# The order of the attention's steps taken from a stored list instead of a planner's rules with shifts

## The chip, the core and the metric

The kernel runs on one core of a Trainium2 chip. The time is the device time of one execution in microseconds (us), the median of three runs. The engines are TensorE (PE, matrix products; its weight loads are shown as PEld), VectorE (DVE), ScalarE (ACT), GpSimd (POOL) and SyncE (SP, which here only issues transfers). TensorE's clock has two levels, 1.2 and 2.4 GHz; the profile gives the granted clock as a share of the upper one.

## What is computed

Attention with mixed heads, and then a feed-forward layer with a softmax gate (SoLU) and a layer norm, over 4 batches, 12 heads, 448 positions, head size 64; the second part has 1792 tokens, 768 to 1024 to 768 channels.

```python
scores = scale * np.matmul(q, k.transpose(0, 1, 3, 2))
scores = np.einsum('bhij,hg->bgij', scores, w_pre)
attn = softmax(scores)                      # maximum, exp, sum + 1e-9, division
attn = np.einsum('bhij,hg->bgij', attn, w_post)
x = np.matmul(attn, v)                      # to (1792, 768)
h = x @ w_in
solu = h * softmax(h)
ln = (solu - mean) / sqrt(var + 1e-6) * g_ln
out = ln @ w_out
```

## The kernel before

Products that need more than fp16 are made of two fp16 halves, `hi` and `lo`. The attention is cut into about 2600 small steps ("tasks"), each with a key. For a batch `b`:

- `ld` loads q, k and v (`raw_q`, `raw_k`, `raw_v`). `am` takes maxima of pieces, `sc` turns them into a power-of-two scale; one step of `sc` is a pair of matmuls, `spread_q` or `spread_k`, that hands a maximum to all partitions. For batch 0 PE transposes (`tp`, line 591, tiles `pt_q`, `pt_k`) and ACT and DVE split (`th`, `tl`); for later batches `hi` (POOL) and `lo` (DVE in two instructions, line 365, or POOL in four, lines 558 and 559) split, and `t` transposes by a transfer (line 571).
- `qk` makes the scores of two heads for a block of 90 or 120 rows (line 644, tile `ps`); `sh` (ACT, line 656) and `sl` (DVE, line 661) copy them to SBUF as halves. Two banks of PSUM hold scores.
- A unit is ten rows of all twelve heads, 45 units a batch. `f` (SP, line 692) fetches a unit into `sr`, with room for four pairs of units. `m`, the premix (line 711, tile `pm`), mixes the heads of a pair of units; `mx` (DVE, line 721) takes the maximum, `ex` (ACT, line 737) the exponential, `gd` and `iv` (DVE) the reciprocal of the sum, `w` (POOL, line 758) the weights `wr`; `o`, the postmix (line 766, tile `po`), mixes again; `po` (ACT, line 369) copies it out.
- `av` (line 815, tile `px`) multiplies by v for two heads; `xh` and `xl` split the result.
- In the last batch `fw` (line 883, tile `cv_wi`) fetches w_in in pieces, `wi`, `wm`, `wh` and `wl` convert it, and `h0` starts the second part.
- 50 `warm` steps of two matmuls each (line 624) compute nothing that is used.

Each task names the engines that can take it, what it needs, and which buffers it takes and frees. `Plan.order()` simulates the engines with fixed costs and due times and gives one list of all tasks; `Plan.shifted()` then moves single tasks in it by the numbers of `SHIFT`. The tasks are written into the program in the order of that list, so each engine gets its own in that order and works through them strictly one after the other; a task that waits holds all that stand behind it on its engine. The second part has a plan of its own, `moe.order()`.

Of the kernel before, what the change touches and what calls it, by code (L numbers as in the profile page):

```python
# [18 lines left out]
class Plan:  # L19
# [34 lines left out]
    4 10 4 -3 1 12 13 1 2 3 -3 3 8 14 2 6 7 1 16 5 24 4 0 3 -11 4 7 9 14 8 9 7 -4 8 16 -5 15 -5 8 9 5 8
    16 -8 -4 15 10 14 15 4 15 1 3 13 22 14 11 14 14 0 8 21 12 20 25 13 11 12 18 4 10 13 16 24 21 0 14 10
    -35 -32 -26 -17 -94 -90 -75 -107 -71 -30 -57 -27 1 -6 0x2 4 -1 5 -1 9 5 -1 4 14 8 17 1 -4 3 4 -9 4
    -8 -3 5 -6 4 -1 7 2 8 5 5 8 5 7 7 -4 7 11 7 -1 12 5 12 13 3 5 14 17 3 4 -71 6 6 -63 -32 -23 -30 -15
    -14 -10 2 -6 1 6 -5 -4 10 11 0 -2 9 2 2 8 8 -4 -4 10 12 1 4 -15 3 -13 -7 -20 0 1 -5 3 -1 2 5 10 -3
    0x2 -3 0 3 8 8 3 -3 -5 2 -2 -1 -7 1 1 1 1 2 0 1 3 0 2 -1 2 2 4 4 0x2 2 -6 3 0 3 -1 2 -1 1 -60 1 1 3
    3 -4 5 5 7 0 3 -3 4 6 0 -5 4 1 -1 -14 1 3 0 3 -1 0 2 2 2 5 9 4 5 -6 -3 -3 2 6 -5 -3 1 1 9 1 1 7 1 1  # L60
    2 5 -4 4 8 -4 3 3 -3 8 9 0 4 0 4 -23 -2 -61 -3 -11 5 0x2 4 -4 4 -2 7 4 7 -4 8 5 -3 -3 -2 4 -9 6 2 6
    -18 1 -8 1 2 2 2 3 -11 0 2 2 2 6 9 -4 -1 -16 2 2 2 5 -6 -6 1 2 -8 -3 1 7 0 2 -4 2 8 -4 -4 -3 -1 1 5
    7 -3 3 3 4 8 -4 -10 -8 3 -1 -8 -2 -2 0x3 2 2 8 1 5 9 10 4 -2 9 -10 -10 20 2 3 4 6 7 -11 1 -8 -13 -17
# [1739 lines left out]
```

## Time and profile before

| | us |
|---|---|
| median of three runs | 652.92 |
| lowest, highest | 652.15, 654.51 |
| span of the profiled execution | 657.9 |

The page gives the profiled execution by its span, from its first to its last instruction; what lies around the span is not listed for it. Its span is 0.8% longer than the median of the timed runs. In the profile "busy" of PE includes matmuls that are under way while they wait for the ones ahead, so a stretch that is 97% busy can still hold time to be had.

### The profile page before, as it was taken

Reading aid. Unit: us, or ns where it says so; the run is one execution under the profiler, and the core shown is the slowest. Engines: PE = TensorE matmul, PEld = TensorE weight load, DVE = VectorE, ACT = ScalarE, POOL = GpSimd, SP = SyncE. Lnnn points to the kernel's source line nnn. Section 1 sums busy time; section 2 is a strip of 40 time slices with the busy share of each in tenths; the row PEclk is TensorE's granted clock in tenths of the full one; section 3 lists DMA queues with packets and bytes.
Section 4 is the critical chain, followed back from the end, with each engine's and each line's share of the span. In section 5 each row is a group of like instructions: output and inputs, shape, how many; then the busy total and the mean of one; then the engine's idle time right before and its main releaser. Section 6 shows DMA issues by size and latency. Waiting matters only on the chain.

```text
span 657.9 us, 17741 instructions
## 1 busy us (share of the span) xinstructions
PE 632.8 (96%) x6660; PEld 433.7 (66%) x6660; DVE 475.1 (72%) x1314; ACT 451.0 (69%) x981; POOL 280.1 (43%) x427
## 2 busy tenths in 40 slices
PE   6889999999999999999899999999999999999997
PEld 6647767777767778778677777774444455666664
DVE  5769998879997689997699999849889896100000
ACT  4679888989888898988799997725455576311111
POOL 2025683235844254593254246404666846300000
PEclk9779999999999999999899999999999999999999
DMA  9037578467677448788746763019964422541211
GB/s 242 12 133 229 178 152 178 156 196 221 204 185 169 150 140 236 234 175 206 219 154 221 214 224 119 3 41 295 186 160 112 97 48 57 113 113 51 64 55 48
DMA packets 114029, 98.53 MB, mean 150 GB/s; under 512 B 69604, under 2 KB 104600, under 8 KB 113944
## 3 DMA queue, kind: packets, MB, share of 16 engines
q1 hardware_dynamic: 108120, 83.62, 45.8%
q0 software_dynamic: 4416, 12.40, 6.9%
q10 hardware_dynamic: 1408, 1.38, 0.8%
q8 instruction: 52, 0.85, 0.5%
q14 instruction: 33, 0.27, 0.1%
HBM read 33.24 MB, written 9.63 MB: 65 GB/s over the span
## 4 chain that ended last, share of the span: by engine, by line
PE 64%; DVE 17%; ACT 7%; DMA 4%; issue 3%; POOL 2%; SPq 1%; ACTq 0%; DVEq 0%; POOLq 0%
PE y L1609 17%; PE po L766 15%; PE ps_h L984 12%; PE px L815 7%; PE ps L644 6%; PE pm L711 6%; DVE dead L721 4%; DVE s L661 3%; ACT e L737 3%; ACT s L656 2%; DMA raw_q<-in_q_dram 2%; DVE hl_k L365 1%; ACT p_t L369 1%; DMA sr<-s 1%; DMA cv_wi<-in_moe_w_in_dram 1%
## 5 line engine op out<-in xcount | busy, mean ns | idle before, releaser
L766 PE MATMUL po<-wr,e 128*112 128x120 f32 x1440 | 176.0, 273 | 6.4 <-POOL wr L758 4.9
L766 PEld LDWEIGHTS po<-wr,e 128*112 128x112 f32 x1440 | 156.8, 178 | 36.8 <-POOL wr L758 15.9
L758 POOL TENSOR_SCALAR wr<-wq,sm 128x120 f32<-128x120 f32 x180 | 77.1, 436 | 186.1 <-DVE sm L752 90.6
L737 ACT ACTIVATE e<-pm,nb,c_exp 128x448 f32<-128x448 f32 x180 | 131.4, 734 | 19.6 <-DVE dead L721 10.2
L721 DVE TENSOR_SCALAR_CACHE_REDUCE dead<-pm,c_nexp 128x448 f16<-128x448 f32 x180 | 121.7, 676 | 14.1 <-PE pm L711 10.1
L661 DVE SCALAR_TENSOR_TENSOR s<-ps,s 120x448 f16<-120x448 f32 (+1 forms) x192 | 112.2, 615 | 16.1 <-ACT s L656 13.8
L369 ACT COPY p_t<-po 112x480 f32<-112x480 f32 x180 | 108.2, 625 | 13.7 <-PE po L766 12.3
L656 ACT ACTIVATE s<-ps 120x448 f16<-120x448 f32 (+1 forms) x192 | 97.3, 552 | 18.1 <-PE ps L644 17.5
L815 PE MATMUL px<-p_t,raw_v 112*64 112x120 f32 (+3 forms) x1632 | 86.8, 259 | 0.8 <-ACT e L737 0.7
L815 PEld LDWEIGHTS px<-p_t,raw_v 112*64 112x64 f32 x1632 | 76.1, 137 | 16.0 <-issue 11.4
L984 PE MATMUL ps_h<-wi,xf 128*128 128x512 f16 x396 | 86.0, 379 | 0.2 <-DVE u L1536 0.2
L644 PE MATMUL ps<-k,q 64*64 64x448 f16 (+2 forms) x1008 | 79.7, 359 | 2.2 <-DVE s L661 1.5
L1609 PE MATMUL y<-wo_h,lth 128*128 128x384 f16 (+2 forms) x224 | 73.0, 326 | 0.0
L1609 PE MATMUL y<-wo_l,lth 128*128 128x384 f16 (+2 forms) x224 | 73.0, 326 | 0.0
L1609 PE MATMUL y<-wo_h,ltl 128*128 128x384 f16 (+2 forms) x224 | 73.0, 326 | 0.0
L984 PEld LDWEIGHTS <-xf 128*128 128x128 f16 x396 | 38.8, 98 | 46.8 <-issue 0.4
L1621 ACT ACTIVATE o<-y,c_out 128x384 f32<-128x384 f32 (+2 forms) x28 | 16.2, 579 | 72.7 <-PE y L1609 72.7
L1609 PEld LDWEIGHTS <-lth 128*128 128x128 f16 x448 | 43.8, 98 | 29.3
L711 PE MATMUL pm<-sr,wp_hi 64*64 64x448 f16 x720 | 57.1, 363 | 4.4 <-DMA sr<-s 2.4
L644 PEld LDWEIGHTS <-q 64*64 64x64 f16 (+2 forms) x1008 | 34.7, 107 | 24.4 <-issue 8.0
L1594 POOL TENSOR_TENSOR ll<-u,lh 128x1024 f16<-128x1024 f32 x14 | 31.4, 2245 | 15.1 <-ACT lh L1590 9.0
L737 ACT ACTIVATION_READ_ACCUMULATOR e<-pm,nb,c_exp 128x1 f32 x180 | 37.6, 209 | 0.0
(182 smaller groups left out, 800.1 us busy)
## 6 DMA issues: line engine op xcount, KB each, us to landing
sr<-s SPq DMA_DIRECT2D x176, 210.0 KB
cv_wi<-in_moe_w_in_dram SPq DMA_DIRECT2D x24, 256.0 KB
cv_wo<-in_moe_w_out_dram SPq DMA_DIRECT2D x8, 768.0 KB
raw_k<-in_k_dram POOLq DMA_DIRECT2D x18, 224.0 KB, 3.7
raw_q<-in_q_dram POOLq DMA_DIRECT2D x18, 224.0 KB, 5.4
raw_v<-in_v_dram POOLq DMA_DIRECT2D x18, 224.0 KB, 3.8
xh<-xsh SPq DMA_DIRECT2D x9, 224.0 KB
xl<-xsl SPq DMA_DIRECT2D x9, 224.0 KB
```

The costliest lines, as they stand in the source:

```text
L369: nc.scalar.copy(out=out, in_=in_)
L644: nc.tensor.matmul(sps[b, c, h + e][lo:hi], q2[b, g][rows, 2 * j + x, i0 + lo : i0 + hi], k1[b, g][rows, 2 * j + y], start=(a == 0), stop= ...
L656: nc.scalar.activation(out=s_t[b, c][0 : y.shape[0], h, 0], in_=y, func=AF.Copy, scale=2.0**-E_S)
L661: nc.vector.scalar_tensor_tensor(out=t[:, h, 1], in0=y, scalar=2.0**-E_S, in1=t[:, h, 0], op0=ALU.mult, op1=ALU.subtract)
L711: nc.tensor.matmul(pmx[b, u + i][64 * e : 64 * e + 64, 0:S], w[rows], sr[b, u][rows, e, z], start=(a == 0), stop=(a == 2),)
L721: nc.vector.tensor_scalar(out=dead, in0=pmx[b, u][:, 0:S], scalar1=c_nexp[0:UK, b : b + 1], scalar2=None, op0=ALU.mult, op1=ALU.min, accum ...
L737: nc.scalar.activation(out=ee[b, u], in_=pmx.pop((b, u))[:, 0:S], func=AF.Exp, bias=nbs.pop((b, u)), scale=c_exp[0:UK, b : b + 1], accum_o ...
L758: ENG[eng].tensor_scalar(out=w, in0=wq[0:UK, 0 : H * UN], scalar1=sm, scalar2=1.0, op0=ALU.mult, op1=ALU.mult)
L766: nc.tensor.matmul(ps[:, c * 120 : (c + 1) * 120], e[:, c * CP : (c + 1) * CP], w, start=True, stop=True)
L815: nc.tensor.matmul(xps[b, blk, g][e * 64 : e * 64 + 64, i, cut], raws["v", b, p][:, e, c * D : (c + 1) * D], next(x for y, x in block_view ...
L984: nc.tensor.matmul(ps[:, n], xx[:, kc, o : o + 128], ww[:, kc, n * 512 : (n + 1) * 512], start=(kc == 0 and a == 0), stop=(kc == KDM - 1 a ...
L1609: nc.tensor.matmul(ys[t, n], lts[t, x][:, kc], w[:, kc, c0:c1], start=(kc == 0 and a == 0), stop=(kc == KFF - 1 and a == 2),)
```

## The change

`SHIFT` is replaced by `ORDER`, a list of 2629 numbers, and `shifted()` by `stored()`: the tasks are sorted by their due times, and each number says which of the tasks that are left comes next; a letter behind it (a, d, p) gives it to ACT, DVE or POOL where it could go to several, otherwise the first engine that the task names takes it. `order()` is no longer used for the attention. The tasks, their instructions, the buffers and the second part's plan are unchanged. Lines below it lie 4 further down, so L766 of before is L770 of after.

```diff
-    SHIFT = """
-    2 2 3 3 3 3 6 7 1 -8 0x2 -12 -9 15 20 16 20 21 21 88 7 -4 1 113 102 32 30 -15 -3 75 17 -9 -13 -13 15
...
+    ORDER = (
+        "99 102 97 95 105 102 102 96 104 2580 2587 2590 108 2595 122 99 101 113 100 96 100 2573 113 118 120 102 114 121 "
...
-    def shifted(self, out):
-
-        moves = []
-        for x in self.SHIFT.split():
-            a, _, n = x.partition("x")
-            moves += [int(a)] * int(n or 1)
-        return [out[i + a] for i, a in enumerate(moves)]
+    def stored(self):
+
+        if not self.ORDER:
+            return [(e, run) for _, e, _, run in self.order()]
+        rest, out = sorted(self.tasks, key=lambda k: self.tasks[k][3]), []
+        for x in self.ORDER.split():
+            n = x.rstrip("adp")
+            run, on = self.tasks[rest.pop(int(n))][:2]
+            out.append(({"a": "act", "d": "dve", "p": "pool"}[x[-1]] if n != x else next(iter(on)), run))
+        return out
...
-        for _, e, _, run in plan.shifted(plan.order()):
+        for e, run in plan.stored():
             run(e)
```

The first place is the head, on PE: the transposes of k and q of batch 0 and the matmuls that spread their maxima. Before, 56 warm matmuls stand ahead of these rows, and then:

```order
L591 MATMUL pt_k_285<-ident_69,raw_k_176 64x112 x8
L591 MATMUL pt_k_294<-ident_69,raw_k_176 64x112 x8
L591 MATMUL pt_k_303<-ident_69,raw_k_176 64x112 x8
L332 MATMUL spread_k_312<-ident_69,amx_k_139 128x128
L591 MATMUL pt_k_314<-ident_69,raw_k_176 64x112 x8
L591 MATMUL pt_k_323<-ident_69,raw_k_176 64x112 x8
L591 MATMUL pt_k_332<-ident_69,raw_k_176 64x112 x8
L332 MATMUL spread_q_377<-ident_69,amx_q_142 128x128
L591 MATMUL pt_q_379<-ident_69,raw_q_181 64x112 x8
L591 MATMUL pt_q_388<-ident_69,raw_q_181 64x112 x8
L591 MATMUL pt_q_410<-ident_69,raw_q_181 64x112 x8
```

In the changed kernel 8 warm matmuls stand ahead, and two to four at each "..." below:

```order
L595 MATMUL pt_k_217<-ident_69,raw_k_176 64x112 x8
...
L595 MATMUL pt_k_237<-ident_69,raw_k_176 64x112 x8
L595 MATMUL pt_k_246<-ident_69,raw_k_176 64x112 x8
L595 MATMUL pt_k_257<-ident_69,raw_k_176 64x112 x8
L336 MATMUL spread_k_266<-ident_69,amx_k_139 128x128
...
L595 MATMUL pt_k_285<-ident_69,raw_k_176 64x112 x8
...
L595 MATMUL pt_k_317<-ident_69,raw_k_176 64x112 x8
...
L595 MATMUL pt_q_334<-ident_69,raw_q_213 64x112 x8
L336 MATMUL spread_q_344<-ident_69,amx_q_142 128x128
L595 MATMUL pt_q_353<-ident_69,raw_q_213 64x112 x8
L595 MATMUL pt_q_362<-ident_69,raw_q_213 64x112 x8
```

The first transpose of q moved ahead of `spread_q`, the fourth of k ahead of `spread_k`, and the rest of the warm matmuls went from the start to places behind score pairs further down, 16 each behind the first two pairs of the second block.

The second place is SP's queue where the last units of batch 2 are fetched (`sr`) and the first rows of w_in (`cv_wi`). Before:

```order
L692 DMA sr_129<-s_3_4689 120x1x896 x2
L883 DMA cv_wi_5520<-in_moe_w_in_dram 128x512
L692 DMA sr_130<-s_3_4689 120x1x896
L883 DMA cv_wi_5520<-in_moe_w_in_dram 128x512
L692 DMA sr_130<-s_3_4689 120x1x896
L883 DMA cv_wi_5520<-in_moe_w_in_dram 128x512 x2
L692 DMA sr_131<-s_3_4689 120x1x896 x2
L692 DMA sr_128<-s_3_4689 120x1x896 x2
```

After:

```order
L696 DMA sr_130<-s_3_4669 120x1x896 x2
L887 DMA cv_wi_5390<-in_moe_w_in_dram 128x512 x3
L696 DMA sr_131<-s_3_4669 120x1x896 x2
L887 DMA cv_wi_5390<-in_moe_w_in_dram 128x512
L696 DMA sr_128<-s_3_4669 120x1x896 x2
L887 DMA cv_wi_5594<-in_moe_w_in_dram 128x512 x4
```

Of the four pieces of the first w_in tile, four stood ahead of the fetch of units 41 and 42 (`sr_131`) and now three do, all behind each other.

The third place is PE in batch 0, from the premix of units 23 and 24 (`pm_23`) to the postmix of unit 23 (`po_23`); `ps` is a score pair, `px` a product with v. Of the rows that repeat one stands here. Before:

```order
L711 MATMUL pm_23_1531<-sr_128,wp_hi 64x448
...
L644 MATMUL ps_3_8_1545<-k_2_364,q_2_485 64x448
...
L815 MATMUL px_1_0_1566<-p_t,raw_v_0_353 64x120 x8
L766 MATMUL po_21_1575<-wr_21_1559,e_21_1474 112x120 x4
L766 MATMUL po_22_1594<-wr_22_1564,e_22_1514 112x120 x4
...
L711 MATMUL pm_25_1599<-sr_129,wp_hi 64x448
...
L644 MATMUL ps_3_10_1623<-k_2_364,q_2_485 64x448
...
L815 MATMUL px_1_0_1566<-p_t,raw_v_1_355 64x120 x8
L815 MATMUL px_1_0_1566<-p_t,raw_v_2_357 64x120 x8
...
L711 MATMUL pm_27_1688<-sr_130,wp_hi 64x448
...
L766 MATMUL po_23_1702<-wr_23_1668,e_23_1589 112x120 x4
```

After:

```order
L715 MATMUL pm_23_1476<-sr_128,wp_hi 64x448
...
L648 MATMUL ps_3_6_1507<-k_1_306,q_1_381 64x448
...
L770 MATMUL po_19_1527<-wr_19_1472,e_19_1385 112x120 x4
L770 MATMUL po_20_1538<-wr_20_1525,e_20_1394 112x120 x4
L770 MATMUL po_21_1557<-wr_21_1503,e_21_1463 112x120 x4
...
L715 MATMUL pm_25_1562<-sr_129,wp_hi 64x448
...
L648 MATMUL ps_3_8_1585<-k_2_346,q_2_430 64x448
...
L819 MATMUL px_1_0_1602<-p_t,raw_v_0_294 64x120 x8
L819 MATMUL px_1_0_1602<-p_t,raw_v_1_309 64x120 x8
L770 MATMUL po_22_1628<-wr_22_1581,e_22_1466 112x120 x4
...
L715 MATMUL pm_27_1639<-sr_130,wp_hi 64x448
...
L770 MATMUL po_23_1680<-wr_23_1637,e_23_1536 112x120 x4
```

The postmixes of units 19 to 22 instead of 21 and 22 now lie between the two, and one product with v fewer; the premixes run further ahead of the postmixes.

On POOL the loads of w_pre and w_post (`rep`) moved ahead of the masks, and on DVE their maximum `am_w` between the two maxima of k's pieces. Of the `lo` steps DVE has 6, 7 and 6 in batches 1 to 3 before, and 7, 5 and 8 after; of `wm` and `wh` as many on each engine as before.

## Rows read from the trace of the kernel before

**Rows 1.** The page: busy us, share of the span, instructions.
```profile
PE 632.8 (96%) x6660; PEld 433.7 (66%) x6660; DVE 475.1 (72%) x1314; ACT 451.0 (69%) x981; POOL 280.1 (43%) x427
```

**Rows 2.** Windows: stretch, its length, busy us by engine, granted clock, DMA share, GB/s.
```profile
16.66:22.04 5.38, 5.38 (x50) 4.88 (x51) 3.36 (x11) 2.68 (x6) 0.00 (x0) 0.50 0.09 25
22.04:36.76 14.72, 12.20 (x122) 6.80 (x121) 12.78 (x31) 11.73 (x30) 2.76 (x10) 0.96 0.00 1
36.76:43.59 6.83, 6.33 (x48) 3.25 (x51) 2.97 (x9) 3.69 (x10) 0.00 (x0) 0.50 0.68 225
...
47.95:442.72 394.77, 384.20 (x5099) 295.06 (x5099) 341.70 (x991) 338.57 (x788) 194.60 (x346) 1.00 0.60 174
442.72:657.90 215.18, 210.75 (x1143) 111.71 (x1141) 100.84 (x231) 84.41 (x130) 77.96 (x50) 1.00 0.45 109
...
263.00:296.00 33.00, 31.82 (x438) 24.86 (x441) 32.07 (x105) 30.68 (x77) 24.73 (x46) 1.00 0.76 204
313.00:320.00 7.00, 4.56 (x59) 3.53 (x58) 4.51 (x17) 5.96 (x14) 2.29 (x6) 1.00 0.92 226
320.00:323.50 3.50, 3.50 (x22) 2.66 (x22) 2.09 (x5) 0.72 (x2) 0.26 (x2) 0.51 0.70 218
```

**Rows 3.** Timeline of PE in the head: start, us, what, idle before and releaser.
```profile
6.83 2.52 PE L591 MATMUL pt_k<-ident,raw_k 112*64 112x112 f32 x48
...
16.66 0.77 PE L332 MATMUL spread_q<-ident,amx_q 128*128 128x128 f32 x2 [4.44 <-DVE amx_q L353]
17.36 4.75 PE L591 MATMUL pt_q<-ident,raw_q 112*64 112x112 f32 x48
...
25.74 1.76 PE L591 MATMUL pt_q<-ident,raw_q 112*64 112x112 f32 x32 [0.87 <-DVE s L661]
...
39.12 1.85 PE L644 MATMUL ps<-k,q 64*64 64x448 f16 x12 [0.39 <-DVE s L661]
...
42.48 0.96 PE L711 MATMUL pm<-sr,wp_hi 64*64 64x448 f16 x8
...
47.94 0.77 PE L766 MATMUL po<-wr,e 128*112 128x120 f32 x5 [0.35 <-POOL wr L758]
```

**Rows 4.** The head on ACT and POOL, and the issues of rep (us to landing last).
```profile
15.39 0.84 ACT L524 ACTIVATE ja_q<-raw_q 112x768 f16<-112x768 f32 x1 [1.22 <-DMA raw_q<-in_q_dram]
...
3.73 0.85 POOL L437 DMA_DIRECT2D rep<-in_w_pre_dram  x1 [0.31 <-POOL rep L435]
...
rep<-in_w_pre_dram POOLq DMA_DIRECT2D x1, 5.6 KB, 7.0
```

**Rows 5.** Waits, whole span: who waited for whom, us, times, longest.
```profile
PEld po L766 <- POOL wr L758: 15.9, 32, 1.1
...
PE po L766 <- POOL wr L758: 4.9, 11, 0.9
```

**Rows 6.** Timeline of PE from 88 to 98 us.
```profile
87.96 0.57 PE L711 MATMUL pm<-sr,wp_hi 64*64 64x448 f16 x8
...
88.55 0.74 PE L644 MATMUL ps<-k,q 64*64 64x448 f16 x12
89.22 1.04 PE L815 MATMUL px<-p_t,raw_v 112*64 112x120 f32 x16
...
91.86 1.07 PE L766 MATMUL po<-wr,e 128*112 128x120 f32 x8 [0.59 <-POOL wr L758]
...
97.74 1.90 PE L766 MATMUL po<-wr,e 128*112 128x120 f32 x16
```

**Rows 7.** Timeline of PE near 320 us, and w_in's issues from 300 to 320.
```profile
320.00 0.93 PE L711 MATMUL pm<-sr,wp_hi 64*64 64x448 f16 x7 [2.44 <-DMA sr<-s]
...
321.24 2.97 PE L766 MATMUL po<-wr,e 128*112 128x120 f32 x16
...
cv_wi<-in_moe_w_in_dram SPq DMA_DIRECT2D x8, 256.0 KB
```

**Rows 8.** Groups of lines: count, busy us, mean ns.
```profile
L365 DVE SCALAR_TENSOR_TENSOR hl_q<-raw_q,p_q,hl_q 112x256 f16<-112x256 f32 x18 | 11.3, 669 | 0.0
```

More of the change, by code (lines that the diff above doesn't have):

```diff
@@ L38 @@
     }
-    SHIFT = """
-    2 2 3 3 3 3 6 7 1 -8 0x2 -12 -9 15 20 16 20 21 21 88 7 -4 1 113 102 32 30 -15 -3 75 17 -9 -13 -13 15
-    -9 16 22 -14 -25 14 23 68 -28 17 63 111 -18 -18 -16 -10 -16 -15 -12 -12 -12 -11 -11 -10 -27 -16 -10
-    -7 0 3 4 -8 -5 2 5 7 0 -12 -20 -9 -2 0 1 2 -13 -8 -13 0x4 2 -1 -9 0 1 -16 -11 1 6 -8 -4 0 11 -9 2 4
[8 rows of a table removed]
-    1 8 0 2 -4 -2 4 -1 5 -15 -11 -7 -4 18 -3 -3 0 4 -3 0 -3 -1 4 0 3 8 4 -3 -6 -4 -2 1 6 -4 0x4 1 -25
-    0x2 2 -1 4 0 5 8 5 9 4 -1 -6 -1 6 6 16 0 4 6 -17 -14 5 1 -8 -2 4 4 7 10 -4 6 -4 9 4 -2 7 3 -29 5 -4
@@ L54 @@
[L54 to L63, printed above, removed]
[12 rows of a table removed]
@@ L76 @@
-    4 -3 0 2 -1 2 2 2 -2 1 -10 2 2 -1 2 -4 -1 1 2 0 4 1 3 0 5 1 2 9 13 -2 -13 1 3 -12 -3 -1 13 0x3 -7 1
-    -12 2 6 14 1 4 5 11 -10 3 4 -7 -11 8 1 -13 3 8 -8 -3 0 -15 2 3 4 -12 -4 3 7 -6 -3 8 -1 0 11 -1 1 11
-    -9 10 -8 5 1 -5 7 15 1 3 -6 7 -14 7 2 9 -14 -14 8 -5 -5 -4 -3 -17 -3 2 2 -4 -3 0 6 0 -2 0 16 0 6 -5
-    -4 -2 13 -2 1 13 -4 0x2 1 -4 8 -3 3 3 -2 -5 7 11 21 7 -21 -19 -2 1 -2 8 4 -6 -3 3 -17 -4 -3 3 11 -1
[13 rows of a table removed]
-    -54 -40 -37 -30 -26 -7 -2 -20 -19 30 1 7 1 -12 0x2 -4 -1 27 2 3 -4 -3 -1 2 -5 -2 17 0 18 0 3 0 3 3
@@ L94 @@
-    -8 -11 1 18 11 13 -8 -2 0 -9 4 6 -1 7 5 8 13 8 15 18 6 3 5 7 -17 9 9 -221 3 9 12 -72 -57 -27 -21 -19
-    -14 -5 -2 0 1 -13 -2 1 4 7 7 -4 6 0x2 5 11 8 8 35 -9 8 -7 7 -14 -1 13 8 -6 -20 -9 -3 4 37 6 -2 -5 6
[14 rows of a table removed]
-    -44 -1 0 1 -8 -7 -5 -1 1 -2 0 4 4 -2 -2 -1 3 0x2 2 4 1 3 0 -11 8 0 -7 9 -2 -2 -1 0 -4 -3 7 15 2 5 9
-    15 -5 -8 -5 10 -1 10 10 10 -8 9 21 22 -18 -14 5 -11 5 -6 -6 1 3 3 12 2 15 3 -20 10 10 13 -3 -1 0 -28
-    -25 8 9 7 14 9 9 -33 4 -8 -3 2 5 11 6 1 3 -15 3 6 9 1 1 -31 7 7 -20 -39 -2 -1 3 -1 3 -6 0 1 2 0 1 1
@@ L113 @@
-    1 1 1 1 1 2 -51 -1 0x11
-    """
+    ORDER = (
[74 rows of a table added]
+    )
     def __init__(self, **rings):
```

120 rows, old and new, of tables (ORDER, SHIFT) are left out of this document.

## The prediction

> **What bounds the kernel now.** I read the busy shares first [rows 1]: TensorE (PE) is busy 96% of the span, VectorE (DVE) 72%, ScalarE (ACT) 69%, GpSimd (POOL) 43%. That is an average over stages, so I cut the span at four events of PE's own timeline [rows 2]: the matmul that spreads q's maximum (16.66 us), the first score matmul (22.04), the first postmix (47.95) and the end of attention (442.72). The reader is to see three things. From 442.72 to the end PE is busy 210.75 of 215.18 us; none of that is reordered, so I leave it alone. From 47.95 to 442.72 PE is busy 384.20 of 394.77: 10.57 us of visible idle is left in the long stretch. And the head, up to 47.95, holds the rest: 4.44 us of idle before one matmul that waits for the maximum of q [rows 3], and two stretches at the lower clock level: 0.50 granted (1.2 GHz) from 16.66 to 22.04 and from 36.76 to 43.59 [rows 2]. The first follows the 4.44 us idle; the second follows a stretch in which PE is busy 12.20 of 14.72 us with pauses. Then I asked who holds PE in the long stretch [rows 5]: POOL's `wr` (the weights that the postmix streams) 4.9 us in 11 waits, while the weight loads of the same postmixes, a row ahead of PE, wait 15.9 us in 32. The longest single wait is 2.44 us at 317, for an `sr` fetch, and the clock then falls to 0.51 from 320 to 323.5 [rows 2, 7].
>
> **The change, part by part.** No instruction's work is new. Of PE's 558 steps 414 stand at another place; by far the most move by a few places only. So the sum is: which of those waits does the new order shorten, and what does it add.
>
> *Head.* (a) The three transposes of q at 17.36 take 4.75 us at the lower clock; the same three of k took 2.52 at the full one [rows 3]. One of three, 4.75/3 = 1.6 us, now stands ahead of `spread_q`, in the idle of 4.44. Saved: 1.6, since PE is busy without a gap from 16.66 to 22.04. (b) Before the transpose at 25.74 PE waits 0.87 us for DVE's score copy [rows 3]; the new order gives ACT and DVE the first heads' pieces of q first and the second pieces later. I take 0.9 as gone; bounds 0 and 0.9. (c) Sixteen warm matmuls each now stand behind two score pairs near 32 to 38 us, where before there were two and four. If that keeps the clock up, the 6.33 us of PE work between 36.76 and 43.59 [rows 2] shrinks to about 3.2 at most; but the score pairs there also wait for DVE (0.39 before one of them [rows 3]), so I take 0.9 out of bounds 0 and 3.1. Head: 1.6 + 0.9 + 0.9 = 3.4; bounds 0 and 5.6. The first premix at 42.48 waits for nothing on PE [rows 3]: PE comes to it late, so what is saved ahead of it is felt.
>
> *What the head's edits cost.* 48 of the 56 warm matmuls ahead of the first transpose are gone. They filled the time up to 6.83 us, in which PE had no data [rows 3]. If the six transposes of k then run at the lower level, they take 2 x 4.75 instead of 2 x 2.52, 4.5 us more, and they have the 4.44 us idle behind them: I cost it at 0, 0.1 without cover left. The weights' maximum, `am_w`, now stands ahead of the second `am_k` on DVE. It waits for `rep`, whose transfer takes 7.0 us from issue [rows 4]; POOL issued it from 3.73 us on, behind the masks, and now issues it ahead of them, at about 2 us, so it lands at 9 to 11, and k's scale, which is ready at 12 now, comes 1 to 1.5 us later. Queued behind are ACT's splits of k. Their cover is that q's last piece lands at 15.39 [rows 4]: 0, and 1.3 if q were early.
>
> The Trainium skill speaks against (a): "TensorE: Matmul & The Clock Gate", Part 1, says that the throttled clock is the default and that activity releases it, so that the missing warm matmuls leave the first transposes cold. The trace agrees that PE's idle precedes the drop at 16.66. By that rule the cost would be the 4.5 us above; by the rows it lies over an idle time of nearly the same length. Its stronger form is a rival below.
>
> *The fetch at 317.* The premix of units 41 and 42 waits 2.44 us for `sr`, and the next two postmixes take 2.97 us instead of 1.90 at the lower clock [rows 6, 7]; with the premix itself (1.24 us from its second matmul to the postmix, where a whole one takes 0.59) that is 4.2 us. On SP's queue four pieces of `w_in` stand ahead of that fetch; now three do. A piece is 256 KB and the DMA engines move 226 GB/s there at a share of 0.92 [rows 2, 7]: 1.2 us less in front. One score pair (0.67 us [rows 6]) now also stands ahead of that premix, where it used to follow. Left: 2.44 - 1.2 - 0.7 = 0.5 us of wait, and I expect the clock to hold over so short a pause for the better part. I take 3.0 of 4.2; bounds 0 (all transfers move up with PE and the queue is as full as before) and 4.2.
>
> *Postmixes with little time.* Between a premix and the postmix of its unit lie a maximum, an exponential, two tiny steps on DVE and POOL's `wr`. PE's own work in between is the cover. I counted it over all 180 units from both orders with the start-to-start times of rows 6: 0.59 for a premix, 0.67 for a score pair, 0.9 for a postmix and an attention-times-v step. Before, 80 postmixes have under 8 us of cover, after it 57, a fall of 29%; the median goes from 8.2 to 8.8 us. At the place shown above the cover of unit 23 goes from 7.7 to 9.2 us, and unit 22's, for whose `wr` PE waited 0.59 us, from 9.0 to 11.2 [rows 6]. What these waits cost lies between the visible 4.9 and the weight loads' 15.9 us [rows 5]; 29% of them is 1.4 to 4.6, and I take the middle, 3.0, since a weight load's wait is partly hidden by the matmuls in flight.
>
> *The low halves of q and k (`lo`).* On DVE one is two instructions of about 0.67 us [rows 8], so 1.3 us. Batch 1 goes from 6 to 7 of them on DVE, batch 2 from 7 to 5, batch 3 from 6 to 8: one more in all, +1.3 us, in stretches where DVE has none to spare (32.07 of 33.00 us at 263 to 296 [rows 2]). I charge 1.3; bounds 0 and 2.6 (batch 3's two, if batch 2 gives nothing back). The swaps of `wm` and `wh` between engines cancel.
>
> *Switches of the tile shape on PE* rise from 289 to 304. A score pair takes 0.67 before an attention-times-v step against 0.59 for a premix before a score pair [rows 6], so one costs at most 0.08, 15 of them 1.2. Counted by neighbours the sum of all PE steps stays within 0.2 us, because a postmix takes about 0.9 whatever follows: 0, at most 1.2.
>
> Sum: -3.4 - 3.0 - 3.0 + 1.3 = -8.1 us. The profiled execution has a span of 657.9; the median of the timed runs is 652.92, 0.8% below it, so part of the waits of that one execution may be its own. Against the span the sum gives 649.8, against the median 644.8; I say 645.0.
>
> **The rivals.** *More is recovered.* All 10.57 us of idle in the long stretch go, with the half-clock stretch at 320 (3.5 us at 0.51, so 1.7) and the head's 3.4: 15.7, that is 637.2. For it: cover grows nearly everywhere. Against it: short covers remain 57 times. *DVE sets the pace.* Then only the head's 3.4 comes, less 1.3: 650.8. For it: DVE at 32.07 of 33.00 us while q and k are prepared; against it: 341.70 of 394.77 over the long stretch [rows 2]. *The clock stays down in the head.* With few warm matmuls at the start PE stays at 1.2 GHz until 36.76. The 12.20 us of work after 22.04, at 0.96 now [rows 2], takes 23.4; the 2.5 us of idle there absorb some, so +8.7; with (a) and (b) kept and the other terms as above: -2.5 + 8.7 - 4.7 = +1.5, so 654.4. It is the skill's rule, taken to its end; against it speaks that the clock was back at 0.96 after 22.04, some 5 us of unbroken PE work behind that idle. *Slower: fetches come late at each batch turn.* In the new order two transposes of k stand back to back on SP ahead of fetches, and one fetch of a pair is parted from the other by transfers; if PE waits for `sr` at all three turns as it does once now, at 4.2 us each, that is +12.6 - 8.1 = +4.5: 657.4. It decides from two and a half such waits on.
>
> **How the numbers follow.** Chances: the forecast (641.5 to 649.6) 0.52, more recovered 0.17, DVE sets the pace 0.16, the clock stays down 0.07, late fetches 0.08. About 0.5%, 3.3 us, is what a measurement of this kernel can tell from no change: faster takes the first two and a little of the third, 0.70; the same the rest of the third and the clock, 0.22; slower 0.08. The range 639 to 654 leaves out half of "more" and the late fetches.
>
> **What would show it.** In the profile after, the first postmix starts at 44.5 (47.94 now); the transposes of q ahead of the first score take about 3.2 us; the granted clock near 37 to 43 is 1.0; no wait for `sr` over 1 us near 317; waits of postmixes for `wr` fall from 4.9 to about 3.5; attention ends at 434 to 436 instead of 442.72, and the stage behind it stays at 215 us. It is wrong if the long stretch stays at 394 us, if a stretch at 1.2 GHz appears outside the head, or if a new wait for DVE stands where `lo` was added.

## The result: slower by 1%

The changed kernel takes 659.43 us (median of 4 runs, 658.7 to 660.51), the kernel before 653.38 (median of 4); the ratio is 1.0096, 95% interval 1.0077 to 1.0115. Its profiled execution has a span of 657.1 us. The one of before had 657.9 [rows 2], but that was a long one: two further profiles of before, below, have 652.7 and 649.8.

The first view of the changed kernel is ACT's timeline in the head (start, us, what, idle before and releaser; ACTq is an issue of a transfer).

```profile
0.81 0.98 ACTq L517 DMA_DIRECT2D raw_k<-in_k_dram  x2
...
5.40 0.32 ACTq L517 DMA_DIRECT2D raw_q<-in_q_dram  x1
6.60 0.84 ACT L528 ACTIVATE ja_k<-raw_k 112x768 f16<-112x768 f32 x1
...
9.09 0.32 ACTq L517 DMA_DIRECT2D raw_q<-in_q_dram  x1
15.37 0.84 ACT L528 ACTIVATE ja_q<-raw_q 112x768 f16<-112x768 f32 x1 [6.88 <-DMA raw_q<-in_q_dram]
...
17.76 0.85 ACT L528 ACTIVATE ja_q<-raw_q 112x768 f16<-112x768 f32 x1
```

Half of the loads of batch 0 are issued by ACT, though the planner lists them as SP's. Two loads of q now stand behind ACT's maxima of k, one behind each, and these wait for k to land. So they go out at 5.40 and 9.09 us, and the last maximum of q comes at 17.76 instead of 15.39 [rows 4].

PE's timeline in the same head shows what follows:

```profile
4.83 1.76 PE L595 MATMUL pt_k<-ident,raw_k 112*64 112x112 f32 x16 [2.37 <-POOL mkp L445]
...
6.85 4.46 PE L595 MATMUL pt_k<-ident,raw_k 112*64 112x112 f32 x48
...
15.33 0.99 PE L595 MATMUL pt_q<-ident,raw_q 112*64 112x112 f32 x16
18.94 0.49 PE L336 MATMUL spread_q<-ident,amx_q 128*128 128x128 f32 x2 [2.62 <-DVE amx_q L357]
19.36 1.75 PE L595 MATMUL pt_q<-ident,raw_q 112*64 112x112 f32 x32
```

The three transposes of k take 4.46 us where they took 2.52 [rows 3], and `spread_q` starts at 18.94 instead of 16.66. Windows of the changed kernel (columns as in [rows 2]):

```profile
18.94:21.50 2.56, 2.41 (x37) 1.97 (x37) 2.46 (x9) 1.75 (x5) 0.00 (x0) 1.00 0.00 0
...
45.00:48.40 3.40, 3.40 (x34) 1.73 (x23) 2.71 (x11) 2.39 (x6) 1.44 (x3) 0.50 0.53 177
47.60:441.92 394.32, 384.94 (x5094) 293.43 (x5091) 340.17 (x988) 338.27 (x782) 193.73 (x339) 1.00 0.61 173
441.92:657.10 215.18, 210.75 (x1143) 111.78 (x1141) 99.61 (x231) 84.39 (x130) 78.04 (x50) 1.00 0.45 109
```

The transposes of q run at the full clock (1.00), as hoped, but a stretch at 0.50 now lies at 45.0 to 48.4, so the first postmix starts at 47.60 (47.94 before). The long stretch takes 394.32 us against 394.77 [rows 2], and the stage behind attention 215.18 both times. PE's longest waits over the whole span (us, times, longest), and its weight loads':

```profile
PE po L770 <- POOL wr L762: 5.2, 9, 1.2
...
PE pm L715 <- DMA sr<-s: 1.8, 3, 1.0
PE spread_v L336 <- DVE amx_v L357: 1.4, 1, 1.4
...
PEld po L770 <- POOL wr L762: 18.1, 37, 1.4
```

The waits for `wr` did not fall: PE waits 5.2 us and its weight loads 18.1, against 4.9 and 15.9 [rows 5]; and a new wait of 1.4 us for v's maximum stands beside them.

### The profile page after: what moved, and what is told of

Same layout as the page of the kernel before. It is cut to its first block, busy times and chain, and to the rows that moved or that the text cites. A ratio compares the mean times of both kernels' runs of the same rounds, so it can differ in the third digit from the quotient of the medians.

```text
span 657.1 us, 17744 instructions
## 1 busy us (share of the span) xinstructions
PE 632.8 (96%) x6660; PEld 429.6 (65%) x6660; DVE 473.6 (72%) x1316; ACT 451.9 (69%) x981; POOL 281.1 (43%) x423
## 4 chain that ended last, share of the span: by engine, by line
PE 65%; DVE 19%; DMA 5%; ACT 5%; issue 3%; POOL 3%; SPq 0%; DVEq 0%; ACTq 0%; POOLq 0%
PE y L1613 17%; PE po L770 16%; PE ps_h L988 12%; PE px L819 8%; PE pm L715 6%; PE ps L648 6%; DVE dead L725 4%; DVE s L665 4%; DMA sr<-s 3%; DMA raw_q<-in_q_dram 2%; ACT e L741 1%; POOL wr L762 1%; DVE xsl L369 1%; DVE u L1540 1%; DVE hl_k L369 1%
## 5 line engine op out<-in xcount | busy, mean ns | idle before, releaser
L770 PE MATMUL po<-wr,e 128*112 128x120 f32 x1440 | 176.4, 273 | 6.3 <-POOL wr L762 5.2
L770 PEld LDWEIGHTS po<-wr,e 128*112 128x112 f32 x1440 | 156.4, 177 | 39.6 <-POOL wr L762 18.1
L741 ACT ACTIVATE e<-pm,nb,c_exp 128x448 f32<-128x448 f32 x180 | 130.7, 729 | 29.2 <-DVE dead L725 13.9
L819 PE MATMUL px<-p_t,raw_v 112*64 112x120 f32 (+3 forms) x1632 | 88.6, 260 | 0.3 <-DVE xsl L369 0.2
L715 PE MATMUL pm<-sr,wp_hi 64*64 64x448 f16 (+1 forms) x720 | 56.5, 361 | 2.2 <-DMA sr<-s 1.8
```

Source lines behind the costliest of these rows:

```text
L715: nc.tensor.matmul(pmx[b, u + i][64 * e : 64 * e + 64, 0:S], w[rows], sr[b, u][rows, e, z], start=(a == 0), stop=(a == 2),)
L741: nc.scalar.activation(out=ee[b, u], in_=pmx.pop((b, u))[:, 0:S], func=AF.Exp, bias=nbs.pop((b, u)), scale=c_exp[0:UK, b : b + 1], accum_o ...
L770: nc.tensor.matmul(ps[:, c * 120 : (c + 1) * 120], e[:, c * CP : (c + 1) * CP], w, start=True, stop=True)
L819: nc.tensor.matmul(xps[b, blk, g][e * 64 : e * 64 + 64, i, cut], raws["v", b, p][:, e, c * D : (c + 1) * D], next(x for y, x in block_view ...
```

## The experiments

In the experiments `stored()` first makes the list `out` of (engine, key), then an edit follows, and then the tasks are taken from it. `old` is the list of before. The table gives the times and, of the profiled execution, the start of the first postmix, the start of batch 0's last postmix (unit 44, found by counting matmuls along PE's timeline), and what follows from there to the end of the span. The runs were made in rounds on different chips (e0 to e3, e4 to e7, e8 to e10, e11 to e14, and e15 with e16), so between rounds the ratios, each to before in its own round, compare better than the times.

| kernel | time, us | ratio to before, 95% interval | first postmix | unit 44 | from there |
|---|---|---|---|---|---|
| before (first profile) | 653.38 | | 47.9 | 137.5 | 520.4 |
| before, e0 | 652.54 | 0.9999 (0.9975 to 1.0022) | 47.0 | 136.4 | 516.3 |
| before, e14 | 651.00 | 0.9996 (0.9974 to 1.0018) | 43.9 | 133.4 | 516.4 |
| changed | 659.43 | 1.0096 (1.0077 to 1.0115) | 47.6 | 134.8 | 522.3 |
| e1, loads first | 656.91 | 1.0071 (1.0046 to 1.0096) | 44.8 | 132.1 | 522.4 |
| e2, weights' maximum back | 659.37 | 1.0106 (1.0080 to 1.0133) | 48.1 | 135.2 | 522.2 |
| e3, both | 656.20 | 1.0058 (1.0037 to 1.0078) | 44.4 | 131.8 | 522.2 |
| e4, new start, old rest | 649.89 | 0.9969 (0.9953 to 0.9986) | 43.3 | 130.6 | 516.8 |
| e16, the same again | 649.87 | 0.9963 (0.9946 to 0.9980) | 43.1 | 130.5 | 517.1 |
| e5, old start, new rest | 658.29 | 1.0084 (1.0053 to 1.0114) | 43.4 | 131.4 | 522.9 |
| e6, engines of before | 671.04 | 1.0302 (1.0268 to 1.0336) | 42.5 | 135.3 | 532.7 |
| e7, v's maximum later | 655.61 | 1.0063 (1.0042 to 1.0084) | 43.3 | 131.6 | 523.1 |
| e8, sums first, 7 places | 664.67 | 1.0176 (1.0145 to 1.0207) | 43.5 | 132.4 | 529.6 |
| e9, e4 with 3 places | 654.55 | 1.0014 (0.9990 to 1.0037) | 43.5 | 130.5 | 520.6 |
| e11, e4, two `lo` on DVE | 651.02 | 1.0003 (0.9988 to 1.0019) | 44.1 | 131.4 | 518.2 |
| e12, e3, two `lo` on POOL | 659.10 | 1.0131 (1.0110 to 1.0153) | 43.9 | 131.2 | 525.7 |
| e13, e4, one exchange | 649.75 | 0.9989 (0.9966 to 1.0013) | 47.0 | 135.7 | 517.3 |
| e15, e13 and POOL's step | 652.18 | 0.9991 (0.9975 to 1.0007) | 43.7 | 132.0 | 518.2 |

e10 (the edit of e8 everywhere) took 702.21 us, a ratio of 1.0750 (1.0716 to 1.0783).

**The head.** The loads, and the maximum of the mixing weights (`mix0`, which waits for the transfer of `rep`), each put back and both:

```diff
+        out.sort(key=lambda x: x[1][0] != "ld" or x[1][2] != 0 or x[1][1] == "v")   # e1, e3
...
+        i = next(i for i, x in enumerate(out) if x[1] == "mix0")                     # e2, e3
+        j = next(j for j, x in enumerate(out) if x[1] == ("sc", "k", 0, 6))
+        out.insert(j, out.pop(i))
```

e0: 

> The kernel before, unchanged, for a second trace of it. The new kernel's executions have a span 1.7 to 2.8 us below their time; the first trace of before has a span of 657.9 us, 5 us above its median time. Theory 1: that trace was an untypical execution, and the clock stages at 1.2 GHz in it (near 320 us above all) and the wait for a fetch at 317 are its own; then this trace has a span of 650 to 653, the first postmix at 44 to 46 us instead of 47.9, and the end of attention at 435 to 437 instead of 442.7. Rival: the trace is typical and the span is no measure here; then the span is again near 658 with the first postmix near 48. Ratio to before 1.000 either way.

e1: 

> The new order, but with the eight loads of k and q of batch 0 first in the list, so that ACT issues its two loads of q ahead of its own maxima of k, as before. Theory 1 (the loads of q that ACT issues at 5.4 and 9.1 us instead of 1.8 to 3.1 hold up the scale of q and all behind it): the matmul that spreads q's maximum goes from 18.9 back to 16.7 or 17, and the time falls by 2 to 2.5 us against the new order, ratio to before 1.0055 to 1.007. Rival 2 (the wait for rep on DVE, ahead of k's second maximum, holds the head): less than 0.5 us, ratio 1.009. Rival 3 (the loss is behind the head): no change in the ratio whatever the head does.

e2: 

> The new order, but with the maximum of the mixing weights behind the scale of k on DVE, as before. Theory 1: q's late loads still decide, so under 0.5 us, ratio 1.009 to 1.0096. Rival 2: k's scale is ready 2 us sooner, and ACT's second maximum of q, queued behind the splits of k, with it: 1 to 2 us, ratio 1.006 to 1.008.

e3: 

> Both edits together. Theory 1: what the loads alone give and up to 1 us more, 2.5 to 3.5 us, ratio 1.004 to 1.006; what is left above 1 is behind the head. If the head explains all of the loss the ratio is 1.000 to 1.002.

ACT's timeline of e3 has both loads of q out by 3.1 us and their maxima at 11.25 and 14.52, with an idle of 2.44 us instead of 6.88:

```profile
1.81 1.29 ACTq L522 DMA_DIRECT2D raw_q<-in_q_dram  x2
...
11.25 0.84 ACT L533 ACTIVATE ja_q<-raw_q 112x768 f16<-112x768 f32 x1 [2.44 <-DMA raw_q<-in_q_dram]
...
14.52 0.85 ACT L533 ACTIVATE ja_q<-raw_q 112x768 f16<-112x768 f32 x1
```

So the late loads cost about 2.6 us of span (657.1 against 654.5 in e1), and 0.25% in the ratios, whose intervals overlap. With the weights' maximum back they cost 3.4 us (657.4 in e2, 654.0 in e3) and 0.48%, with intervals that just stay apart; part of it is the clock, which is low for 6.8 us in e2's profile and for 3.4 in e3's. The weights' maximum costs nothing while q is late (e2) and 0.5 us of span once q is early (e3 against e1), which the intervals can't tell from nothing. The Trainium skill, "DMA: Bandwidth & Descriptors", section "Issuing engines are not separate DMA queues", says that spreading issues over engines saves only the time that the issuing takes, which is usually small. This trace differs in what it can cost: where the issuing engine also computes, its issue stands behind a wait; here ACT's two loads of q went out by 3.1 us in e3, and at 5.40 and 9.09 in the changed kernel.

Even so e3 is slower than before, so the head isn't the main loss. The third profile of before tells what the head of before is worth:

e14: 

> The kernel before, unchanged, for a third profile of its head. In two of its profiles the granted clock is 0.50 to 0.64 from about 36 to 43 us; in the kernel with the old start and the new rest, whose head has the same instructions, it stays at 1.00 and the first postmix stands at 43.4 instead of 47.0 and 47.9. If the low clock belongs to the order of the head, the first postmix stands at 47 to 48 here too; if it comes and goes by execution, anything from 43.4 to 48.

Rows of PE's timeline in e14, then windows of PE (busy us, count, granted clock, DMA share, GB/s) in e14, and then in e5, whose head has the instructions of before:

```profile
14.77 0.46 PE L332 MATMUL spread_q<-ident,amx_q 128*128 128x128 f32 x2 [2.27 <-DVE amx_q L353]
...
17.61 0.77 PE L644 MATMUL ps<-k,q 64*90 64x448 f16 x6
```

```profile
36.00:40.00 4.00, 4.00 (x40) 0.50 0.68 233
40.00:45.00 5.00, 4.14 (x56) 0.92 0.32 111
```

```profile
36.00:40.00 4.00, 3.72 (x50) 1.00 0.68 231
```

The same instructions got half the clock there in three profiles of four. With the new start it fell somewhere between 16 and 50 us in the changed kernel, e2, e3 and e13, and stayed up in the eleven others. The clock isn't all that varies: q's maximum was spread at 14.77 us in e14, 15.72 in e0 and 16.66 in the first profile. The first postmix of one and the same head stands between 43.4 and 47.9 us, and one profile can't show a gain of 3 us in the head.

**Start against rest.** The list is cut behind unit 44 of batch 0:

```diff
+        cut = next(i for i, x in enumerate(out) if x[1] == ("o", 0, 44)) + 1   # e4, behind both edits of e3
+        done = {k for _, k in out[:cut]}
+        out = out[:cut] + [x for x in old if x[1] not in done]
...
+        cut = next(i for i, x in enumerate(old) if x[1] == ("o", 0, 44)) + 1   # e5
+        done = {k for _, k in old[:cut]}
+        out = old[:cut] + [x for x in out if x[1] not in done]
```

e4: 

> The order of both corrections up to the postmix of unit 44 of batch 0 (the last postmix of the first batch but a few), every remaining step in the order and on the engines of before. Theory 1: the new order gains in the head and in batch 0 and loses in batches 1 to 3; then this postmix stands at 131.8 us as in the kernel with both corrections, and from there on the 516.3 us of before follow: span 648.1 against 652.7, time about 648, 0.7% under before. Rival: the new order is early at this point only because it put other work off, which then has to be done; span 652 to 654, time that of before.

e5: 

> The reverse: before's order and engines up to the postmix of unit 44 of batch 0, the remaining steps in the new order on the new engines. Theory 1: 136.4 us to that postmix and then the 522.2 us that the kernel with both corrections takes from there; span 658.6, time about 658, 0.9% over before. Rival (work put off): the new order from there on costs nothing by itself; time 652 to 653.

e16: 

> The kernel with the new start and the old rest, unchanged, a second time, for its interval against before: if the gain of 0.3% is real, a ratio of 0.995 to 0.999; if it was chance, 0.999 to 1.001.

Windows of all engines from unit 44 to the end, in e0, e4, e3 and e5:

```profile
136.43:652.69 516.26, 506.06 (x5098) 339.80 (x5096) 362.12 (x988) 343.31 (x735) 225.33 (x302) 1.00 0.54 148
```

```profile
130.61:647.41 516.80, 506.54 (x5094) 339.56 (x5092) 362.32 (x986) 343.30 (x733) 224.58 (x302) 1.00 0.54 148
```

```profile
131.78:654.04 522.26, 509.31 (x5094) 339.43 (x5092) 364.01 (x986) 345.80 (x733) 226.49 (x302) 1.00 0.54 146
```

```profile
131.45:654.30 522.85, 509.67 (x5098) 340.17 (x5096) 363.99 (x988) 346.14 (x735) 226.63 (x302) 1.00 0.53 146
```

This is the clearest result of the study. Whatever the start, the old rest takes 516.3 to 517.3 us behind unit 44 (520.4 in the first profile of before, with its wait of 2.44 us for `sr` [rows 7]), and the new rest 522.2 to 522.9. The new order of batches 1 to 3 costs 5 to 6.5 us at a granted clock of 1.00 in all four, and no work was merely put off. The new start with the old rest beats before: 0.9969 and 0.9963. (e13, which differs from it by an exchange that moved nothing on PE, has 0.9989 with an interval that reaches 0.9966, so the gain may be nearer to 0.2%.)

The clock bears on this gain. Every timed execution has its span and its mean granted clock on record. Of 112 executions of before in the five rounds, 10 had a mean clock of 0.998 or more; their spans are 646.3 to 648.1 us, with a median of 647.7. Of the 24 of e4 and e16, 22 had it; their spans are 647.1 to 648.7, with the same median. So at the same clock the new start with the old rest is no faster than before. What it gains is that the clock falls in fewer executions.

Where does the new rest lose? I cut it into nine stretches of equal PE work (30 us of PE's steps each). They take 284.8 us in e4 and 289.4 in e3; PE's idle time in them grows from 5.8 to 8.5 us, and the rest of the loss lies in time that is counted as busy. Two of the stretches differ by 1.5 us each, and the ones ahead of them by 1.0 and 0.9: these are windows of e4 and then of e3 (all engines; PE, PEld, DVE, ACT, POOL).

```profile
256.60:289.56 32.96, 32.10 (x434) 24.59 (x432) 31.78 (x105) 30.70 (x77) 24.68 (x47) 1.00 0.77 205
289.56:319.96 30.40, 30.10 (x426) 24.27 (x426) 24.28 (x69) 27.32 (x62) 10.97 (x23) 1.00 0.84 242
319.96:351.73 31.77, 30.85 (x426) 23.63 (x424) 29.78 (x78) 29.61 (x69) 16.76 (x21) 1.00 0.56 185
```

```profile
258.74:293.27 34.53, 31.89 (x427) 24.45 (x427) 34.04 (x110) 31.06 (x76) 24.37 (x45) 1.00 0.80 209
...
324.60:357.84 33.24, 31.78 (x418) 24.24 (x416) 31.53 (x79) 30.68 (x71) 13.50 (x20) 1.00 0.56 179
```

Over all nine DVE is busy 254.9 us in e4 and 254.6 in e3: the same. But in the first of these stretches it is busy 34.04 of 34.53 us in the new order. The groups of DVE's lines in that stretch, of e4 and then of e3, say with what:

```profile
L459 DVE SCALAR_TENSOR_TENSOR hl_k<-raw_k,p_k,hl_k 112x256 f16<-112x256 f32 x8 | 4.3, 588 | 0.0
L459 DVE SCALAR_TENSOR_TENSOR hl_q<-raw_q,p_q,hl_q 112x256 f16<-112x256 f32 x4 | 2.4, 631 | 0.0
...
L620 DVE TENSOR_REDUCE am_q<-raw_q 112x1 f32<-112x768 f32 x2 | 1.9, 944 | 0.0
```

```profile
L374 DVE SCALAR_TENSOR_TENSOR hl_k<-raw_k,p_k,hl_k 112x256 f16<-112x256 f32 x8 | 5.2, 686 | 0.0
L374 DVE SCALAR_TENSOR_TENSOR hl_q<-raw_q,p_q,hl_q 112x256 f16<-112x256 f32 x8 | 4.7, 622 | 0.0
L535 DVE TENSOR_REDUCE am_q<-raw_q 112x1 f32<-112x768 f32 x4 | 3.7, 942 | 0.0
```

Two more `lo` (four instructions) and two more maxima stand in it, and each half of k takes 0.1 us longer. The Trainium skill, "Perfetto Trace Analysis", section "Identifying the Most-Contended Engine", takes the occupancy of VectorE as a fair measure of how near it is to its limit; the section behind it adds that the engine in question can change from one regime to the next. This trace agrees with the second: over the span TensorE is the busiest (96%, VectorE 72% [rows 1]), in this stretch VectorE (99%, TensorE 92%). Whether 99% is a limit here is what e11 and e12 were to test.

**How much work, or on which engine?**

```diff
+        eng = {k: e for e, k in old}                     # e6: e3, 27 steps back on their engines
+        out = [(eng[k], k) for _, k in out]
...
+        two = [("lo", "q", 3, 4), ("lo", "q", 3, 5)]     # e11: in e4 to DVE; e12: in e3 to POOL
+        out = [("dve" if k in two else e, k) for e, k in out]
```

e6: 

> Both corrections and the new order, but each of the 27 steps that changed its engine is on the engine of before. As predicted (one more low half of q and k on VectorE costs 1.3 us) the time falls from 656.2 to about 654.9. Rival 1: the engine of these steps doesn't matter, 655.7 to 656.7. Rival 2: the new order needs its own choice of engines, because a step that GpSimd takes at over twice VectorE's duration comes late where the new order wants it; then the time rises to 657.5 or more.

e11: 

> The kernel with the new start and the old rest (649.9), and the low halves q.3.4 and q.3.5 on VectorE, where the new order has them, instead of GpSimd, at the same place of the list. In the stretch in which q and k of the last batch are prepared VectorE is busy 31.78 of 32.96 us there. Theory 2 (VectorE sets PE's pace in that stretch, whatever the order): four more instructions of 0.63 us and their room, 1.4 us of it left, so 1.2 to 2.6 us more, time 651.1 to 652.5. Rival: the order of the steps is what costs, not how much VectorE has to do; 649.4 to 650.4.

e12: 

> The reverse: both corrections and the new order (656.2), and the low halves q.3.4 and q.3.5 on GpSimd as before. VectorE is busy 34.04 of 34.53 us in that stretch, GpSimd 24.37. Theory 2: VectorE loses 2.5 us of work there and 1 to 2 us come back, time 654.2 to 655.2. Rival: GpSimd also makes wr, which then stands behind 2.4 us of a low half; what VectorE gives back is lost to wr, 655.7 to 658.

Two `lo` more on DVE cost the old rest 1.1 to 1.4 us behind unit 44 (518.2 against 516.8 and 517.1) and 0.34% in the ratio to e4's, with intervals apart; against e13, on the same chip, it is 0.14%, and the intervals overlap. The loss isn't in the full stretch, which takes 32.96 us as in e4, but in the one behind it, where most of the added work ran and DVE is far from full:

```profile
257.50:290.46 32.96, 31.75 (x434) 24.77 (x433) 32.31 (x105) 30.66 (x77) 24.29 (x45) 1.00 0.78 206
290.46:322.00 31.54, 30.74 (x426) 24.57 (x426) 25.58 (x73) 27.48 (x63) 7.40 (x16) 1.00 0.82 237
```

That stretch takes 1.14 us more than e4's, with DVE busy 25.58 of 31.54 us. So e11 gives a price, but it doesn't show that a full DVE sets it. Taken off DVE in the new order the two cost 3.5 us instead of giving any back, more than even the rival had (659.1, where it went to 658). My theory fell there. The stretch in e12, its waits (1.2 us for `wr` in e3's) and POOL's timeline:

```profile
258.08:296.12 38.04, 33.58 (x428) 25.89 (x427) 34.01 (x111) 32.31 (x78) 29.05 (x53) 0.96 0.83 195
```

```profile
PE po L777 <- POOL wr L769: 3.0, 3, 1.8
```

```profile
290.08 0.48 POOL L569 TENSOR_SCALAR raw_q<-raw_q,p_q 112x256 f32<-112x256 f32 x1
290.64 0.67 POOL L570 TENSOR_TENSOR hl_q<-raw_q,hl_q 112x256 f16<-112x256 f32 x1
291.29 0.71 POOL L769 TENSOR_SCALAR wr<-wq,sm 128x120 f32<-128x120 f32 x2
```

`wr` stands behind a row of POOL's halves. (Part of this stretch ran at the lower clock, 0.96 in the mean; the medians, 659.10 against 656.20, say the same.) In e6 it happens at many places, though a `lo` takes POOL 2.3 us by these rows and DVE 1.2 to 1.4, which is not quite the "over twice" of the expectation: PE waits 13.9 us for `wr` from 131 to 440 us, against 5.4 in e3, and the time is 14.8 us longer. The new order can't do without its own choice of engines; the old order with all of the new engines was not run.

**One late step at a time.** Each delay that PE shows has a step that seems to hold it. Four edits move such steps:

```diff
+        scale = [("sc", "v", 2, n) for n in range(1, 8)]    # e7: the spread of v's maximum
+        j = next(j for j, x in enumerate(out) if x[1] == ("m", 2, 21))
+        late = [x for x in out[:j] if x[1] in scale]
+        out = [x for x in out[:j] if x[1] not in scale] + [out[j]] + late + out[j + 1 :]
...
+            for e, k in out[j:i + 1]:                       # e8, e9, e10: from ("mx",) + g to ("iv",) + g
+                t = self.tasks[k]
+                if e == "dve" and k[0] in ("lo", "wi") or any(a in [y for _, y in late] for a in t[2] + t[7]):
+                    late.append((e, k))
+                else:
+                    kept.append((e, k))
+            out = out[:j] + kept + late + out[i + 1 :]
...
+        i = next(i for i, x in enumerate(out) if x[1] == ("iv", 3, 34))   # e13, e15
+        j = next(j for j, x in enumerate(out) if x[1] == ("wm", 4))
+        out.insert(j, out.pop(i))
+        i = next(i for i, x in enumerate(out) if x[1] == ("wi", 5, 5))    # e15 only
+        j = next(j for j, x in enumerate(out) if x[1] == ("w", 3, 35))
+        out.insert(j, out.pop(i))
```

e7: 

> Both corrections and the new order; only the matmul that spreads the maximum of v for batch 2 stands four PE steps later, behind the premix of units 21 and 22. Theory 1: the 1.4 us that PE waits for VectorE's amx_v there is lost to the end; the wait goes and the time falls from 656.2 to about 654.8. Rival: the wait is only where a late chain shows first; the next postmix then waits about as long for wr, and the time stays within 0.5 us of 656.2.

e8: 

> Both corrections and the new order; at seven pairs of units (1.22, 1.28, 2.17, 2.19, 2.21, 3.10, 3.32, at which PE is held longest past its own steps: 1.1, 0.73, 0.64, 0.89, 0.78 and 1.37 us at the six with a visible delay, 5.5 in all) the low halves and the conversions of w_in that stand on VectorE between the maximum and the reciprocal of the sums go right behind the reciprocal. Theory 1: the order of VectorE's steps between a unit's exponential and its reciprocal makes wr late; most of the 5.5 us comes back, the time falls from 656.2 to 652 or 653. Rival: VectorE is only busy there; what is put behind the reciprocal makes the next unit late by as much, 655.5 to 656.7.

e9: 

> The kernel with the new start and the old rest (649.9), and there the same edit at the three places with the longest delays: units 1.18 (0.80 us), 1.20 (0.98) and 3.34 (1.02, where a maximum of w_in, 1.21 us, stands between the two steps of the sums). Theory 1: 2 to 2.8 us come back, time about 647.4. Rival (the delay only moves to the next unit): within 0.7 us of 649.9.

e10: 

> Both corrections and the new order, the same edit at every pair of units of batches 1 to 3. Theory 1 in its strong form: the sums' two steps want to stand ahead of all background work; then the time is 650 to 652. Rival: background work that is pushed back everywhere comes late for its own users (transposes of k and q, the stage behind attention), time 656 or more.

e13: 

> The kernel with the new start and the old rest (649.9) with one pair of VectorE's steps exchanged: the reciprocal of units 34 and 35 of batch 3 ahead of the maximum of w_in's fifth piece (1.21 us), which stands between the two steps of the sums now. PE is held 1.02 us there. If that delay is lost to the end, 648.9; if it moves to the next unit, 649.9.

e15: 

> The kernel with the new start and the old rest, the exchange on VectorE, and GpSimd's conversion of w_in's piece 5 (2.40 us) behind the wr of units 34 and 35 instead of ahead of it. Theory 3 (what held PE there was GpSimd's own step ahead of wr, not the reciprocal): the delay of 1.02 us in front of unit 34's postmix falls under 0.3 and attention, from the postmix of unit 29 of batch 3 on, takes about 1 us less than the 41.6 us of the kernel without the edits. Rival: VectorE's maximum of that piece now waits for GpSimd and with it the next units' maxima; the 1 us is lost one unit later and the stretch stays at 41.6.

In e7 the wait for v's maximum is gone, the waits for `wr` grow from 5.4 to 6.2 us, and the time is that of e3 within the interval. In e8 the waits of postmixes for `wr` do halve (5.4 us in e3), but the score matmuls now wait for DVE's copies and for a transfer that transposes q; PE's waits over the whole span:

```profile
PE ps L665 <- DVE s L682: 4.1, 9, 2.7
PE po L787 <- POOL wr L779: 2.7, 6, 1.3
...
PE ps L665 <- DMA q<-hl_q: 1.8, 1, 1.8
```

Seven edits meant to win 3 to 4 us lost 8; in e9, meant to win 2 to 2.8 us, the span grew by 3.7 (PE's waits of 1.20 us for v's maximum and 2.32 at unit 34 took the place of 0.91 at unit 20 of batch 1 and 0.95 at unit 34); and everywhere it cost 46 us. The pair e13 and e15 shows why, at one place. First e13, DVE and POOL:

```profile
403.17 2.40 POOL L1014 TENSOR_TENSOR wi<-cv_wi 128x1024 f32<-128x1024 f32 x1
403.25 0.17 DVE L849 RECIPROCAL sm<-sm 128x2 f32<-128x2 f32 x1
...
405.55 0.71 POOL L855 TENSOR_SCALAR wr<-wq,sm 128x120 f32<-128x120 f32 x2
```

The reciprocal is ready at 403.42, but POOL has just begun a conversion of w_in, and `wr` starts when that ends, at 405.55: PE waits 0.95 us there, as in e4 without the exchange. In e15 the conversion stands behind `wr`:

```profile
399.86 0.37 POOL L858 TENSOR_SCALAR wr<-wq,sm 128x120 f32<-128x120 f32 x1 [0.42 <-DVE sm L852]
...
400.96 2.40 POOL L1017 TENSOR_TENSOR wi<-cv_wi 128x1024 f32<-128x1024 f32 x1
...
403.40 1.22 DVE L1041 TENSOR_REDUCE am_wi<-wi 128x1 f32<-128x1024 f32 x1 [1.20 <-POOL wi L1017]
...
404.96 0.35 PE L432 MATMUL spread_wi<-ident,amx_wi 128*128 128x128 f32 x1 [1.84 <-DVE sm L848]
```

`wr` follows its reciprocal at once. But the conversion now ends at 403.36, DVE waits 1.20 us for it, and PE waits 1.84 us at the spread of w_in's maximum. From unit 29's postmix to the last one it takes 32.2 us, against 31.2 in e4, e16 and e13. Theory 3 was right about the place; on the time its rival was nearer, though it expected no change and 1 us was lost.

## Why the prediction was wrong

**The head, term (a), failed at its cover.** I took "q's last piece lands at 15.39" as fixed and looked for changes in the orders of PE and DVE; that two of q's loads stand in ACT's own stream, behind its maxima of k, I did not see. In place of 1.6 us saved, `spread_q` came 2.3 us later. With the loads put back it starts at 15.7 (e3). The 1.6 itself was mis-sized too: from `spread_q` to the first score matmul it now takes 2.54 us instead of 5.38, but in e14, with the old order and the clock up, it takes 2.84. So by these two profiles the transpose that moved ahead is worth 0.3 us, and the rest is the clock. Term (b) came: no wait over 0.2 us for DVE's score copy is left there. The cost of the weights' maximum was rightly 0 under late q. With q early `spread_q` comes 1.7 us later by it (17.37 in e1, 15.70 in e3), of which 0.5 is seen in the span; e3's profile has 3.4 us at the lower clock near 42 us that e1's has not, so the price is not settled.

**The head, term (c), named a real effect, but the changed kernel didn't get it whole.** There the clock did stay up from 36.8 to 43.6, and fell from 45.0 to 48.4 instead. In one profile that looks like chance, since such stretches come and go with the execution, in before as well. Over all their timed executions the new start with the old rest has a mean clock of 0.999, before 0.994, and at the same clock its gain is gone; the four executions of the changed kernel, with q late, have 0.994 to 0.997. That the warm matmuls behind the score pairs keep the clock up, as I had it, isn't shown, since the new start differs in more. The rival of a clock that stays down in the head did not come: the slow transposes of k were over at 11.3 us, and the clock is 1.00 from 11 us to 45.

**The fetch at 317 was no term at all.** The 3.0 us belonged to one execution: neither e0 nor e14 has that wait, and they take 4 us less behind unit 44. I saw that the profiled execution was 0.8% over the median and still summed over its waits.

**"Postmixes with little time" is the step that failed most.** I counted PE's own work between a premix and its postmix, and it did grow: the mean distance over 180 units went from 8.77 us (e0) to 9.65 (changed). But the steps in between grew with it: from the premix to the end of `wr` 7.40 us before, 8.16 after. The time that is left between the end of `wr` and its postmix fits the result better, though no run varied it alone: in batch 0 it grew from 1.2 to 1.7 us in the mean, and there the new order gained; behind unit 44 it stayed at 1.4. A longer order on PE doesn't help if DVE, ACT and POOL come to their steps later too. Predicted were 3.0 us saved; the new rest lost 5 to 6.5.

**`lo` on DVE** came near its size by luck. I charged 1.3 us for one more in all; in e11 the two more of the last batch cost 1.1 to 1.4 us of span, in the old order and behind the stretch in which DVE is full, so that the place was wrong. "DVE sets the pace" is the rival nearest in kind, since the gain behind the head failed to come, but I priced it only as that, and e12 speaks against it. "Late fetches" is nearest in time (657.4) and did not occur: the longest wait for `sr` is 1.0 us. By its own prices it would have taken 2.7 such waits, not two and a half.

The sum, from the third profile of before to the changed kernel (649.8 to 657.1): the first postmix 3.7 us later (43.9 to 47.6; late loads and the clock), from there to unit 44 2.3 us less (89.5 to 87.2), behind it 5.9 us more. Shown by a run: the split at unit 44, the late loads, the price of two `lo` in the old order. Open: which of the many other moved steps behind unit 44 make up the other 4 to 5 us. In two stretches DVE holds more work, but that this is the cause isn't shown, and every single step that I moved away only moved the delay.

## What to carry to other kernels

Read a new order on every engine that issues, not on the engine that the plan names: a load on an engine that also computes goes out when that engine gets there. Don't count a step's cover in one engine's work; follow the whole chain, with the queue of each engine on it, in the stretch in question, and ask where the most loaded engine is full there. And where an order was searched as a whole, don't mend single waits in it: cut it between stages and join the better halves, as the new start with the old rest, which was 0.3 to 0.4% faster than before in two comparisons. And before a gain is put down to an order, compare executions at the same granted clock: this one was gone there.
